# Attention and a state-space layer on one core: fifteen late rotations off TensorE, their first half on ScalarE or GpSimd, the sum on GpSimd

## The chip, the cores and the metric

The kernel runs on one core of one Trainium2 chip. The metric is the time of one execution in device microseconds (us), as the median of several runs; a profile of one execution is taken beside it. TensorE (PE) multiplies matrices into PSUM, VectorE (DVE), ScalarE (ACT) and GpSimd (POOL) work on elements, SyncE (SP) issues transfers. Each engine works off its own queue in order, and semaphores order the engines among themselves.

## The reference

Two layers run on inputs of 2048 tokens by 448 features, and their outputs are put side by side. The first is attention with 16 heads of 28 features, in which a token sees itself and seven tokens at steps of two behind it. The second is a linear recurrence with 448 complex states (S5).

```python
def _A_ref(x, wqkv, wo):
    ...
    logits = jnp.einsum("bhsd,bhswd->bhsw", q, kg) * scale
    attn = _softmax(logits, axis=-1)
    o = jnp.einsum("bhsw,bhswd->bhsd", attn, vg)
    return (o, transposed and flattened) @ wo

def _B_ref(x, Lambda_re, Lambda_im, B_re, B_im, C_re, C_im, log_dt, Dskip):
    Lam_bar = jnp.exp(dt * Lam)
    Bu = jnp.einsum("bld,pd->blp", x + 0j, B_bar)
    for t in range(L):
        h = Lam_bar[None, :] * h + Bu[:, t, :]
        hs.append(h)
    y = 2.0 * jnp.einsum("blp,dp->bld", hseq, Cmat).real + x * Dskip
```

## The kernel before

The order of all work is written out by hand in the string ORDER (from L32): 559 steps such as `W_30@0` or `z52.`. A loop at the end of the kernel calls a function for each. The digits are its arguments, the digit behind @ is the PSUM bank (one of eight), and a last `.` or `=` says whether ScalarE or VectorE copies a result out of PSUM (all these copies go through the helper at L114). A step stands in the queue of the engine that runs it at its place in ORDER, so ORDER sets the queues of all engines.

Attention comes first: projections (QK, QS, V_), products of queries and shifted keys on VectorE (P, L372: two tensors in SBUF), their sums by head on TensorE (E_), softmax (sma, smb, smc). The weights are laid out as bands: AL shifts them on TensorE, `al` copies them into Ak0 or another buffer, `ad` writes them to DRAM and `sp` reads them back skewed into PT. AV multiplies PT with the values (L505), `av` copies the result, W_ multiplies with wo (L518), `w` copies and `ow` stores.

The recurrence treats its 448 complex states as seven groups g of 64, real parts in 64 partitions and imaginary parts in the other 64. Time is cut in blocks of four tokens (j = 0 to 3). BU multiplies inputs with B, BR and UP carry the state inside a block (z and y copy out of PSUM; z takes j, and j = 3 goes to the tile Z3, the others to Z). A scan over blocks follows on VectorE, two groups at a time: `sa` turns the phase (products of tensors in SBUF), `sb` scans, `sd` turns back. DN and `dn` (L754) then finish the even blocks of the group. From these block states the states at j = 0, 1, 2 are made by a rotation: the state before the block, times a complex number that differs by state, is added to Z[g, j]. It is done in one of two ways:

- on TensorE: H_(j, g), a matmul with a rotation matrix (L761), and `h` (L766), by which VectorE adds the result in PSUM to Z[g, j];
- off TensorE, for the nine rotations of groups 4, 5 and 6: `sw(g)`, two transfers (L784, L785), puts a copy of the states with real and imaginary halves exchanged into what is left of BT. Then VectorE makes `ha` or `ka` (L790), t = state x cosine part + Z, into one of five F32 buffers that lie in Ak0, and `hb` or `kb` (L794), Z = exchanged state x sine part + t. The two names of each half are the same code. Both halves read two tensors in SBUF.

C(j, ct) (L825) multiplies Z or Z3 for a quarter ct of the blocks with Cw, over all seven groups, so a C with j below 3 needs all seven rotations of its j. `c` (L831) adds x times Dskip (made by `xd`, L815, in xnB) and empties the bank; `oc` stores. CH is the half of one C, and comes with ch and oh. Cw is scaled on the way by `ca` (ScalarE, L657) and `cs` (VectorE, L661).

On ScalarE the steps `ts` make sine tables, `tx` and `smb` use the exponential. PT is cleared by GpSimd (L895), whose last work are four small copies (L773, step pk).

Of the kernel before, what the change touches and what calls it, by code (L numbers as in the profile page):

```python
# [10 lines left out]
F32 = mybir.dt.float32  # L11
ALU = mybir.AluOpType
ACTF = mybir.ActivationFunctionType
# [16 lines left out]


ORDER = """  # L32
WU@0 XI0@12 xi30. xi20. PP@3 pcopy xi00= pa pb XI1@45 xi31. pd_ xi01. tf3 xi21. pc QS10@6 ts03 pe XH1@7 xh1. qk010.
XA11@3 xa11. tf0 ts13 XA10@2 xt1 ts23 pf xa10= QS00@1 qk000= P000 QK050@04 QK031@57 ts00 QK021@26 QK051 qk050. qk051.
QK061@13 QK060 qh011. pg ts10 qh001. QK030 tf1 ts01 QK020 qk020. QS01@0 qk030= ts20 QK041@45 qh000= V_011@12 P001
QK040 ts11 qk031. qk021. ts21 qk040. tf5 ts05 V_010 V_100@76 qh010. QS11@4 tf4 ts15 P040 P021 v010. P041 v011. xt2
qk041. P020 ts25 tz ts04 V_101 qk001. V_111@31 v101. rb0 V_001@25 V_000 P030 v001. V_110 v110. rb3 QK110@06 v000.
qk011. E_00@5 P050 E_02 E_04 P031 v111. QK161@32 v100. ts14 QK111 qk111. P010 QK121@41 hc0 QK160 qk110. tf6 qh111.
QK120 QK130@76 qh110. QK100@02 ts06 QK101 QK131 ts16 qk121. qk120. qh101. qk101. P011 E_01@1 E_03 P060 P051 E_05
V_401@42 qk130= P061 ts24 qh100. qk100. QK141@73 E_06 QK140 lt01 tf2 qk131. P100 V_400 lt00 ts26 xt3 P130 qk140. ts02  # L40
BD v400. P111 TR0@0 P131 P110 v401. tr0. V_410@16 qk141. V_500@57 xt0 ts12 V_511@42 V_501 V_411 QK151@03 v410. P101
v500. QK150 V_510 P120 v411. hc1 OZ v501. ts22 qk150. E_10@1 E_11@5 sma0 E_13 qk151. BU301@67 v510. v511. BU401@03
BU201@42 BU300 BU200 P121 P151 smb0 LC z30. P140 BR31 XR ci3. z20. P141 ci0. BU400 ci1. CD1 BR21 BU000@64 z21. E_12
z40. E_14 z31. ci2. P150 E_15 BU311@20 P160 P161 BU001 smc0 E_16 lt10 lt11 BU310 BR32 TR1@7 CD2 z00. BR01 z32. tr1.
BU210@15 BR41 xd1 CD3 BR33 BU101@62 sma1 z41. CD0 OP pm0 BU211 AL0@7 al0. BU100 pm3 smb1 ad0 xd3 pm1 z33= BR22 z10.
z22. BU500@37 z01. BR11 z11. BU010@61 smc1 UP3 BU011 wo ca6 tx rb1 BU501 BU111@42 y3= z50. BR02 z02= ca3 BU110 sp0 cs3
xd2 BR12 z12. BR23 AL1@3 z23. al1. BR03 z03. BR13 z13. ad1 pm4 AL2@0 al2. cs6 UP2 y2. BR51 z51. AL3@6 UP1 xd0 y1= al3.
UP0 y0. ca1 BU410@43 BU611@05 BU601@76 BU411 ad2 BU511@21 sa0 BR42 BU600 ca4 BU510 z60. BR52 pm2 cs1 sb0 z42. BR43
BR61 sd0 BU610 DN0@7 sp1 z43. UP4 z52. BR53 z61. ca0 sa2 BR62 z62. AV010@4 y4. z53. av010. AV031@2 AV020@6 rb2 cs4
av031. AV000@0 av020. av000. ad3 AV021@3 AV001@4 av021. sp2 AV011@2 AV030@6 dn0 av030. H_00@7 av001. W_30@0 av011.  # L50
BR63 UP5 sb2 H_20@3 pk H_10@6 W_31@4 y5. W_01@2 sd2 cs0 h20 w31. DN2@1 sp3 w30. W_21@3 h10 z63. w01. w21. ca2 ca5
W_10@4 DN3@6 W_20@0 ow30 UP6 ow01 w10. sa4 y6. dn3 AV131@2 sb4 AV101@3 av101. AV120@6 dn2 AV100@1 ow21 AV130@4 AV110@5
w20. AV111@3 ow31 sd4 h00 ow10 sa6 AV121@0 av120. sb6 sd6 av110. DN5@7 ow20 av111. W_11@6 av121. av131. DN1@5 dn1
H_13@3 W_61@0 av100. dn5 H_12@2 w61. W_51@1 cs2 cs5 sw5 ow61 H_22@5 h13 w11. ha25 DN6@7 W_00@0 ow11 av130. DN4@6 h22
W_70@4 H_11@3 dn4 sw4 ha15 w51. H_03@1 w00. dn6 C32@0 c32 ow00 ha26 W_50@5 hb25 w50. W_40@6 W_71@7 H_21@0 ha16 w70.
W_41@5 ow51 w40. ow70 h11 ha14 W_60@4 h12 ow40 sw6 w41. ow41 h03 hb15 w71. hb14 h21 C30@6 hb16 H_02@3 H_23@5 ow71 h23
ka04 hb26 C33@7 ha24 hb24 C13@2 H_01@1 h01 w60. c33 oc32 C31@4 kb04 oc33 c31 C10@0 C11@5 c11 ka05 oc31 C22@1 c22 h02
c30 ka06 C20@7 ow50 oc11 kb05 ow60 C21@4 kb06 C12@5 c20 oc30 oc20 oc22 c12 C03@1 c21 c10 oc21 oc12 C02@3 oc10 c13 oc13
C01@6 c03 oc03 c01 c02 C00@7 c00 CH1@5 oc01 oc02 CH0@4 oc00 ch1 oh1 ch0 oh0
"""  # L60

@with_exitstack
def kernel(
# [17 lines left out]
    V = nc.vector  # L81
    ACT = nc.scalar
    PE = nc.tensor
    POOL = nc.gpsimd
# [5 lines left out]
    def pool(name, side="left", bufs=1, c=ctx):  # L90
        return c.enter_context(tc.tile_pool(name=name, bufs=bufs, side=side, reuse_waits="tile"))
# [129 lines left out]
    Ak0 = smp.tile([128, 2, 2560], BF16, tag="Ak0")  # L221
# [7 lines left out]
    pp = {}  # L229
# [301 lines left out]
    def small(name, *shape):  # L531
        return const.tile([128, *shape], F32, tag=name, name=name)
# [72 lines left out]
    BT = keep.tile([128, G, 4, 128], BF16, tag="BT")  # L605
# [162 lines left out]
    co2 = small("co2", 2, T - 1, G)  # L768
# [9 lines left out]
    def prev(g, a=0, b=128):  # L778
        s = late["Z3"][a:b, g, OD - 1:OD - 1 + N2]
        return bass.AP(s.tensor, s.offset, [list(s.ap[0]), [EV - OD + 1, 2], [1, N2]])  # L780
# [3 lines left out]
        SP.dma_start(swp(g)[0:64], prev(g, 64, 128))  # L784
        SP.dma_start(swp(g)[64:128], prev(g, 0, 64))  # L785

    def rot_a(e, j, g):
        t = pp["ht", j, g] = Ak0.rearrange("p k n -> p (k n)").bitcast(F32)[:, 512 * (late["k"] % 5):512 * (late["k"] % 5) + 512]
        late["k"] += 1
        e.scalar_tensor_tensor(t.rearrange("p (a n) -> p a n", a=2), prev(g), co2[:, 0, j, g:g + 1],  # L790
                               late["Z"][:, g, j, :].rearrange("p (a n) -> p a n", a=2), ALU.mult, ALU.add)

    def rot_b(e, j, g):
        e.scalar_tensor_tensor(late["Z"][:, g, j, :], BT[:, g].rearrange("p b n -> p (b n)"), co2[:, 1, j, g:g + 1],  # L794
                               pp.pop(("ht", j, g)), ALU.mult, ALU.add)

    @op
    def ha(j, g):
        rot_a(V, j, g)

    @op
    def hb(j, g):
        rot_b(V, j, g)

    @op
    def ka(j, g):
        rot_a(V, j, g)

    @op
    def kb(j, g):  # L810
        rot_b(V, j, g)

    @op
    def xd(cb):
# [47 lines left out]
    late = {}  # L862
# [12 lines left out]
    @op  # L875
    def OP():
        cl.close()
        s6 = pool("a_pt")
        for n, shape in (("PT", (NS, H // HS, PW)), ("oT", (2, 4, 2, 512)), ("wo", (4, D)), ("ya", (6, D))):
            late[n] = s6.tile([128, *shape], BF16, tag=n, name=n)  # L880

        late["Ak"] = [Ak0[:, 0], Ak0[:, 1], late["oT"][:, 1].rearrange("p a b n -> p (a b n)")[:, 0:2560],
                      late["ya"].rearrange("p k n -> p (k n)")[:, 0:2560]]
        late["n"] = 0
        late["k"] = 0

    @op
    def pm(i):
# [14 lines left out]
    for step in ORDER.split():  # L903
        name, args, bank, e = re.fullmatch(r"([A-Za-z]+_?)(\d*)@?(\d*)([.=]?)", step).groups()
# [33 lines left out]
```

## Time and profile before

| | |
|---|---|
| median of 3 runs | 130.98 us (130.95 to 131.43) |
| the profiled execution | 131.52 us, of which the span from first to last instruction is 129.8 us |
| granted clock of TensorE | 1.000 |
| rotations as matmuls, L761 | 12 of 128x512, 4.1 us busy, 0.215 us apart |
| their sums, L766 | 12, 8.1 us busy, 686 ns each |
| first halves, L790 | 9, 6.7 us busy, 746 ns each |
| second halves, L794 | 9, 6.6 us busy, 749 ns each |
| GpSimd | 23.0 us busy, nothing after 73.6 us until the end |
| swap to landing (L784, L785) | 2.1 us |

Busy times are of one profiled execution; an instruction's duration overlaps the next one's by some 0.09 us on VectorE and by more on TensorE, so busy times are above what a queue takes at full speed. A chain of waits is the work that ended last, followed back from the end.

### The profile page before, as it was taken

To read this page: it belongs to the slowest core of one execution; us is meant where nothing else is said; L and a number is where in the kernel's file an instruction comes from. 1 tells how busy PE (TensorE), PEld (TensorE's weight loads), DVE (VectorE), ACT (ScalarE), POOL (GpSimd) and SP (SyncE) were. 2 spreads that over 40 slices of the span, in tenths; PEclk is the share of its full clock that TensorE was granted. 3 is DMA by queue.
4 is the path that set the end of the run, shared out by engine and by line. 5 is a ranking of instruction groups with operands and counts; after the bars stand their busy time and mean duration, and the time that the engine had idled before them with its cause. 6 is when DMAs were issued, how large, how long until landed. Compare 5 with 4: busy or idle time off the path is not lost.

```text
span 129.8 us, 2885 instructions
## 1 busy us (share of the span) xinstructions
PE 122.5 (94%) x1067; PEld 63.4 (49%) x1078; DVE 119.5 (92%) x213; ACT 89.3 (69%) x183; POOL 23.0 (18%) x45
## 2 busy tenths in 40 slices
PE   6889999999999999999999996999999999999990
PEld 6742434434335434434536342955965554555560
DVE  5797999999999999999999999978999999999981
ACT  3589889888879899987899989859997250000000
POOL 6808000000000000037899600000000000000000
PEclk9999999999999999999999999999999999999999
DMA  3899998999999999566458989958211354015272
GB/s 111 201 314 280 310 191 168 224 225 241 159 230 210 216 171 345 205 123 128 165 168 144 326 232 261 219 106 186 99 56 36 110 170 123 7 41 172 83 235 71
DMA packets 44981, 22.91 MB, mean 177 GB/s; under 512 B 31335, under 2 KB 43943, under 8 KB 44967
## 3 DMA queue, kind: packets, MB, share of 16 engines
q1 hardware_dynamic: 44904, 22.72, 74.1%
q8 instruction: 8, 0.13, 0.5%
q14 instruction: 6, 0.05, 0.1%
q10 hardware_dynamic: 63, 0.01, 0.0%
HBM read 11.56 MB, written 6.29 MB: 138 GB/s over the span
## 4 chain that ended last, share of the span: by engine, by line
PE 79%; DMA 7%; ACT 6%; DVE 2%; issue 2%; SPq 1%; ACTq 0%; DVEq 0%
PE ps L238 32%; PE ps L825 15%; PE ps L518 9%; PE ps L505 6%; PE ps L384 4%; DMA pd<-Ak 3%; DMA PT<-pd 3%; PE ps L256 2%; PE ps L761 2%; ACT ctmp L657 2%; PE ps L695 1%; ACT Z L114 1%; PE ps L845 1%; SPq L474 1%; PE ps L341 1%
## 5 line engine op out<-in xcount | busy, mean ns | idle before, releaser
L372 DVE TENSOR_TENSOR pr<-qf,kf 128x2048 bf16<-128x2048 bf16 x24 | 28.0, 1219 | 0.3
L238 PE MATMUL ps<-xbuf,BT 128*128 128x512 bf16 (+1 forms) x108 | 23.4, 380 | 0.4 <-issue 0.3
L238 PE MATMUL ps<-xT,wq 128*128 128x512 bf16 (+1 forms) x92 | 20.5, 380 | 0.5 <-issue 0.2
L825 PE MATMUL ps<-Cw,Z 128*128 128x448 bf16 x105 | 20.6, 353 | 0.0
L114 ACT CAST Z<-ps 128x512 bf16<-128x512 f32 (+1 forms) x31 | 14.8, 525 | 1.3 <-PE ps L695 1.1
L825 PEld LDWEIGHTS <-Z 128*128 128x128 bf16 x105 | 10.3, 98 | 10.0 <-DVE Z L794 0.4
L238 PEld LDWEIGHTS <-BT 128*128 128x128 bf16 (+1 forms) x112 | 8.9, 97 | 12.0 <-issue 2.9
L518 PE MATMUL ps<-wo,oT 128*128 128x448 bf16 x64 | 13.7, 353 | 0.0
L238 PEld LDWEIGHTS <-wq 128*128 128x128 bf16 (+1 forms) x96 | 7.6, 97 | 11.6 <-issue 3.6
L895 POOL MEMSET PT<- 128x4320 f32 x3 | 11.1, 3702 | 10.2 <-PE ps L388 10.2
L238 PE MATMUL ps<-wq,xT 128*128 128x448 bf16 (+1 forms) x64 | 12.4, 353 | 0.0
L114 ACT CAST ya<-ps 128x448 bf16<-128x448 f32 (+1 forms) x17 | 8.7, 551 | 5.2 <-PE ps L518 3.6
L114 ACT CAST oT<-ps 128x512 bf16<-128x512 f32 x17 | 9.1, 621 | 1.1 <-PE ps L505 1.1
L505 PE MATMUL ps<-PT,v_s 128*32 128x135 bf16 (+1 forms) x256 | 8.7, 299 | 1.2 <-DMA PT<-pd 1.2
L657 ACT ACTIVATE ctmp<-Cw,c2t 64x448 f32<-64x448 bf16 x14 | 9.3, 666 | 0.2
L831 DVE TENSOR_TENSOR xbuf<-ps,xnB 128x448 bf16<-128x448 f32 x15 | 8.7, 618 | 0.4 <-PE ps L825 0.4
L518 PEld LDWEIGHTS <-oT 128*128 128x128 bf16 x64 | 6.3, 98 | 5.5 <-ACT oT L114 0.2
L766 DVE TENSOR_TENSOR Z<-ps,Z 128x512 bf16<-128x512 f32 x12 | 8.1, 686 | 0.9 <-PE ps L761 0.9
L114 ACT CAST v_s<-ps 128x448 bf16<-128x448 f32 x16 | 7.9, 547 | 1.0 <-PE ps L238 0.9
L238 PEld LDWEIGHTS <-xT 128*128 128x128 bf16 (+1 forms) x64 | 5.4, 97 | 5.8 <-issue 1.2
L505 PEld LDWEIGHTS <-v_s 128*32 128x32 bf16 x256 | 7.0, 111 | 1.9 <-issue 1.5
L114 ACT CAST qf<-ps 128x512 bf16<-128x512 f32 x11 | 6.4, 592 | 0.8 <-PE ps L238 0.7
(159 smaller groups left out, 199.6 us busy)
## 6 DMA issues: line engine op xcount, KB each, us to landing
PT<-pd SPq DMA_DIRECT2D x16, 156.0 KB, 3.9
xnB<-in_B_x_dram SPq DMA_DIRECT2D x2, 896.0 KB
out_dram<-ya SPq DMA_DIRECT2D x16, 112.0 KB, 1.8
out_dram<-xbuf SPq DMA_DIRECT2D x15, 112.0 KB, 1.7
pd<-Ak SPq DMA_DIRECT2D x2, 640.0 KB, 5.3
xbuf<-in_A_x_dram SPq DMA_DIRECT2D x2, 448.0 KB
xnB<-in_B_x_dram SPq DMA_DIRECT2D x4, 224.0 KB, 5.8
xnB<-in_B_x_dram SPq DMA_DIRECT2D x4, 192.0 KB, 4.5
```

The costliest lines, as they stand in the source:

```text
L114: (ACT.copy if e == "A" else V.tensor_copy)(o, i)
L238: PE.matmul(o, l, r, start=(first and i == 0), stop=(not first and i == len(pairs) - 1 and not more[s]))
L256: PE.matmul(p[:, 0:128], wz[:], wz[:], start=True, stop=True)
L372: V.tensor_tensor(t[:], q.unsqueeze(1).to_broadcast((128, 4, 512)), k4, ALU.mult)
L384: PE.matmul(acc[s][32 * i:32 * i + 32], E[:, f, ws, :], t[:, i, :], start=(f == 0 and ws == 0), stop=False)
L505: PE.matmul(p[32 * hh:32 * hh + 32, 128 * bl:128 * bl + n], v_s[:, t, 4 * hg + hh, :], PT[:, t % NS, (4 * hg + hh) // HS, (4 * hg + hh) % ...
L518: PE.matmul(p[:, 0:D], late["oT"][:, b // 4, hg, par, 128 * (b % 4):128 * (b % 4) + 128], late["wo"][:, hg, :], start=(hg == 0), stop=(hg ...
L657: ACT.activation(t[a:a + 64, 0:D], Cw[b:b + 64, g, :], ACTF.Copy, scale=c2t[a:a + 64, g:g + 1])
L766: V.tensor_tensor(zz, pp.pop(("h", j, g))[:], zz, ALU.add)
L825: PE.matmul(p[:, 0:D], z, Cw[:, g, :], start=(g == 0), stop=(g == G - 1))
L831: V.tensor_tensor(yo, pp.pop(("c", j, ct))[:, 0:D], xnB[:, ct, j, :], ALU.add)
L895: POOL.memset(late["PT"][:, 4 * i:4 * i + 4].rearrange("p t g n -> p (t g n)").bitcast(F32), 0.0)
```

## The change

Fifteen rotations instead of nine are made off TensorE: those of groups 2 to 6. Groups 0 and 1 stay on TensorE. A rotation off TensorE is now three steps: its first half is a product alone, by ScalarE (`ga`, groups 4 to 6) or by GpSimd (`gp`, groups 2 and 3); GpSimd adds Z to it in place (`gb`); VectorE makes the second half (`hb`) as before. Two more pairs of `sw` transfers are issued. A buffer now belongs to its rotation by the order in which first halves stand in ORDER, still five in turn.

```diff
-    def rot_a(e, j, g):
-        t = pp["ht", j, g] = Ak0.rearrange("p k n -> p (k n)").bitcast(F32)[:, 512 * (late["k"] % 5):512 * (late["k"] % 5) + 512]
-        late["k"] += 1
-        e.scalar_tensor_tensor(t.rearrange("p (a n) -> p a n", a=2), prev(g), co2[:, 0, j, g:g + 1],
+    def ht(j, g):
+        if (j, g) not in hts:
+            hts[j, g] = Ak0.rearrange("p k n -> p (k n)").bitcast(F32)[:, 512 * (len(hts) % 5):512 * (len(hts) % 5) + 512]
+        return hts[j, g]
+
+    @op
+    def ha(j, g):
+        V.scalar_tensor_tensor(ht(j, g).rearrange("p (a n) -> p a n", a=2), prev(g), co2[:, 0, j, g:g + 1],
                                late["Z"][:, g, j, :].rearrange("p (a n) -> p a n", a=2), ALU.mult, ALU.add)
...
     @op
     def hb(j, g):
-        rot_b(V, j, g)
...
+        V.scalar_tensor_tensor(late["Z"][:, g, j, :], BT[:, g].rearrange("p b n -> p (b n)"), co2[:, 1, j, g:g + 1],
+                               ht(j, g), ALU.mult, ALU.add)
+
+    @op
+    def ga(j, g):
+        ACT.activation(ht(j, g).rearrange("p (a n) -> p a n", a=2), prev(g), ACTF.Copy, scale=co2[:, 0, j, g:g + 1])
+
+    @op
+    def gp(j, g):
+        POOL.tensor_scalar(ht(j, g).rearrange("p (a n) -> p a n", a=2), prev(g), co2[:, 0, j, g:g + 1], 1.0, ALU.mult, ALU.mult)
+
+    @op
+    def gb(j, g):
+        POOL.tensor_tensor(ht(j, g), ht(j, g), late["Z"][:, g, j, :], ALU.add)
```

`ha` stays defined and is not called. ORDER is replaced as a whole. By count of its steps: H_ and h 12 to 6; ha and ka 9 to 0; hb and kb 9 to 15; gp 6, ga 9 and gb 15 are new; sw 3 to 5. Copies that change their engine: al0, al1, al3, av030, av130, v000, w31, w40, w70, xa11, xi21, y5, z01, z03 and z50 go from ScalarE to VectorE; qh000, qk030, qk130, xa10, y1, y3 and z33 go the other way. The steps ts05, ts15 and ts25, which make the last sine table, now stand late, ts15 and ts25 behind tx. The late part of the new order, from the first AV (every rotation of groups 2 to 6 lies in it):

```
AV000@7 AV030@0 av030= AV020@4 av000. z62. cs1 y4. AV010@7 av010. AV001@6 AV011@2 AV021@3 z53. AV031@7 UP5 av001.
av020. y5= av011. DN3@6 dn3 BR63 W_00@4 sp2 W_10@2 av031. av021. W_11@0 z63. gp23 gb23 DN2@7 sa4 dn2 sb4 W_31@3 w31=
w00. gp13 w10. W_30@5 UP6 ca4 cs4 W_01@6 w11. ca0 gp12 w30. W_21@4 sp3 AV111@2 gp22 gb12 cs0 AV110@7 AV100@0 AV101@3
av111. sd4 y6. sw3 ca2 gp03 gb03 AV121@5 sa6 av121. ow10 AV130@2 av130= av101. ow00 ow11 sb6 AV131@1 av110. AV120@5
DN4@3 ow30 gb22 gb13 av131. DN5@2 W_51@7 hb23 ca5 W_61@1 av120. ow31 dn4 cs2 W_20@3 av100. sw2 dn5 hb12 W_71@2 w20.
hb13 hb03 w51. cs5 w71. H_11@5 ow51 h11 W_70@0 H_21@3 ow20 w70= sw5 W_40@7 sd6 ga15 gb15 ow71 ow70 W_41@2 ga05 C32@5
w01. h21 w61. sw4 H_01@6 hb22 gb05 H_10@0 C33@1 w40= w41. ow41 DN6@2 ga14 h10 dn6 ga16 h01 hb15 H_00@3 ga24 C31@7
W_60@0 gb14 hb14 h00 W_50@2 ow01 sw6 hb05 c32 ga26 w60. gb16 oc32 ga04 gb24 H_20@6 ow60 hb16 gb26 ga25 C30@0 ow40
C10@3 w21. gb25 xd1 w50. ow50 hb24 C11@5 C12@4 c31 hb26 c10 C13@2 oc31 hb25 ga06 gb06 oc10 h20 CH1@7 c12 C21@3 oc12
gb04 ow61 xd3 c30 hb04 gp02 oc30 C22@6 gb02 C20@4 c21 c11 oc21 oc11 hb02 c33 ch1 oh1 hb06 C00@0 c00 oc33 c20 oc20 c22
c13 C03@3 C02@5 oc00 c03 oc13 oc03 C01@1 ow21 c02 oc02 c01 oc22 oc01 CH0@7 ch0 oh0
```

In the order before, the first AV was AV010, and ha25, the first half rotation off TensorE, stood behind h13 near the middle of the same part; H_13, H_12, H_22, H_03, H_02 and H_23 stood between DN1 and C33.

More of the change, by code (lines that the diff above doesn't have):

```diff
@@ L32 @@
 ORDER = """
[L33 to L57, printed above, removed]
@@ L58 @@
-c30 ka06 C20@7 ow50 oc11 kb05 ow60 C21@4 kb06 C12@5 c20 oc30 oc20 oc22 c12 C03@1 c21 c10 oc21 oc12 C02@3 oc10 c13 oc13
-C01@6 c03 oc03 c01 c02 C00@7 c00 CH1@5 oc01 oc02 CH0@4 oc00 ch1 oh1 ch0 oh0
+WU@0 XI0@12 xi00= xi20. xi30. PP@3 pcopy pa pb XI1@45 xi01. xi21= xi31. QS10@6 qk010. XA11@7 pc pd_ tf3 pe xa11=
+XA10@1 XH1@3 QS00@2 qk000= xa10. xh1. P000 QS01@0 P001 pf QK050@45 pg rb1 qk001. QK051 tf6 QK031@67 qk050. ts03
+QK021@13 ts13 ts23 QK041@20 BD QK040 qk040. P040 tf0 qk041. QK030 qk030. qk051. QK020 qk020. QS11@4 QK061@20 V_111@65
@@ new lines @@
+ts06 ts16 ts26 ts00 qk011. P041 QK060 qh010. P020 ts10 V_110 P021 qk021. v110. v111. P011 V_100@14 tz tf1 E_00@3
+qk031. E_02 E_04 qh011. V_011@65 ts20 rb3 qh001. V_101 v101. V_001@70 V_000 v001. V_010 v100. ts01 QK110@40 v010.
+QK111 qh000. QK161@16 P010 v011. qk111. v000= P050 ts11 ts21 qk110. QK121@72 QK160 tf2 xt3 qh110. qh111. QK120
+QK100@50 hc0 QK130@46 qh101. QK101 qk121. qh100. P031 hc1 QK131 tf4 ts04 xt0 qk100. E_01@2 qk130. xt2 P030 qk120.
+qk101. ts02 E_03 P051 E_05 V_410@15 V_411 P061 rb0 qk131. QK141@47 QK151@06 P060 E_06 lt00 P101 ts12 lt01 QK150 P110
@@ new lines @@
+ts22 v411. qk151. QK140 TR0@3 qk140. V_500@25 tr0. V_501 v410. P131 tf5 xt1 P100 ts14 ts24 v501. qk150. V_401@64 v500.
+V_511@31 V_510 v511. v510. pk P130 V_400 LC P111 E_11@5 E_10@0 E_13 sma0 BU301@21 qk141. v400. P120 P150 BU401@37
+v401. BU201@64 BU300 ts05 smb0 XR OZ z30. BU200 z20. BU400 ci0. P151 BR31 P141 ci1. z31. P140 z40. P121 BU000@26 BR21
+E_12 E_14 z21. E_15 BU311@13 ci3. BU001 P160 P161 E_16 BU310 smc0 CD3 BR32 ci2. lt10 lt11 TR1@4 CD0 z00. tr1. BR01
+z01= sma1 BU210@05 BU211 BU101@24 AL0@6 BU100 al0= CD2 rb2 z32. BR33 smb1 BR41 z10. BR22 CD1 OP pm0 z22. smc1 BU010@16
@@ new lines @@
+ad0 BR11 ca6 z41. pm3 wo BU500@20 BU501 pm1 cs6 BU011 z50= z11. BU111@74 BU110 BR12 ca3 xd0 BR02 sp0 z33. z12. BR51
+z02= AL1@2 BR23 BR13 UP3 z23. BR03 z13. y3. pm4 tx al1= AL2@7 UP1 y1. z03= AL3@1 ad1 UP0 UP2 al2. y0. xd2 ts15 al3=
+BU410@23 BU601@47 BU411 sa0 z51. cs3 y2. BU611@61 ad2 BU511@05 sb0 sd0 ca1 BU600 z60. BR42 z42. BU510 BR61 BR43 sa2
+BR52 BU610 DN0@4 ts25 z43. sp1 DN1@2 dn0 UP4 z61. ad3 BR62 sb2 dn1 sd2 z52. pm2 BR53 AV000@7 AV030@0 av030= AV020@4
+av000. z62. cs1 y4. AV010@7 av010. AV001@6 AV011@2 AV021@3 z53. AV031@7 UP5 av001. av020. y5= av011. DN3@6 dn3 BR63
@@ new lines @@
+W_00@4 sp2 W_10@2 av031. av021. W_11@0 z63. gp23 gb23 DN2@7 sa4 dn2 sb4 W_31@3 w31= w00. gp13 w10. W_30@5 UP6 ca4 cs4
+W_01@6 w11. ca0 gp12 w30. W_21@4 sp3 AV111@2 gp22 gb12 cs0 AV110@7 AV100@0 AV101@3 av111. sd4 y6. sw3 ca2 gp03 gb03
+AV121@5 sa6 av121. ow10 AV130@2 av130= av101. ow00 ow11 sb6 AV131@1 av110. AV120@5 DN4@3 ow30 gb22 gb13 av131. DN5@2
+W_51@7 hb23 ca5 W_61@1 av120. ow31 dn4 cs2 W_20@3 av100. sw2 dn5 hb12 W_71@2 w20. hb13 hb03 w51. cs5 w71. H_11@5 ow51
+h11 W_70@0 H_21@3 ow20 w70= sw5 W_40@7 sd6 ga15 gb15 ow71 ow70 W_41@2 ga05 C32@5 w01. h21 w61. sw4 H_01@6 hb22 gb05
@@ new lines @@
+H_10@0 C33@1 w40= w41. ow41 DN6@2 ga14 h10 dn6 ga16 h01 hb15 H_00@3 ga24 C31@7 W_60@0 gb14 hb14 h00 W_50@2 ow01 sw6
+hb05 c32 ga26 w60. gb16 oc32 ga04 gb24 H_20@6 ow60 hb16 gb26 ga25 C30@0 ow40 C10@3 w21. gb25 xd1 w50. ow50 hb24 C11@5
+C12@4 c31 hb26 c10 C13@2 oc31 hb25 ga06 gb06 oc10 h20 CH1@7 c12 C21@3 oc12 gb04 ow61 xd3 c30 hb04 gp02 oc30 C22@6 gb02
+C20@4 c21 c11 oc21 oc11 hb02 c33 ch1 oh1 hb06 C00@0 c00 oc33 c20 oc20 c22 c13 C03@3 C02@5 oc00 c03 oc13 oc03 C01@1
+ow21 c02 oc02 c01 oc22 oc01 CH0@7 ch0 oh0
@@ L785, in sw @@
         SP.dma_start(swp(g)[64:128], prev(g, 0, 64))
-    def rot_a(e, j, g):
-        t = pp["ht", j, g] = Ak0.rearrange("p k n -> p (k n)").bitcast(F32)[:, 512 * (late["k"] % 5):512 * (late["k"] % 5) + 512]
-        late["k"] += 1
[L790 to L795, printed above, removed]
+    def ht(j, g):
+        if (j, g) not in hts:
+            hts[j, g] = Ak0.rearrange("p k n -> p (k n)").bitcast(F32)[:, 512 * (len(hts) % 5):512 * (len(hts) % 5) + 512]
+        return hts[j, g]
+    hts = {}
     @op
     def ha(j, g):
-        rot_a(V, j, g)
+        V.scalar_tensor_tensor(ht(j, g).rearrange("p (a n) -> p a n", a=2), prev(g), co2[:, 0, j, g:g + 1],
+                               late["Z"][:, g, j, :].rearrange("p (a n) -> p a n", a=2), ALU.mult, ALU.add)
     @op
     def hb(j, g):
-        rot_b(V, j, g)
-    @op
-    def ka(j, g):
-        rot_a(V, j, g)
-    @op
-    def kb(j, g):
-        rot_b(V, j, g)
+        V.scalar_tensor_tensor(late["Z"][:, g, j, :], BT[:, g].rearrange("p b n -> p (b n)"), co2[:, 1, j, g:g + 1],
+                               ht(j, g), ALU.mult, ALU.add)
+    @op
+    def ga(j, g):
+        ACT.activation(ht(j, g).rearrange("p (a n) -> p a n", a=2), prev(g), ACTF.Copy, scale=co2[:, 0, j, g:g + 1])
+    @op
+    def gp(j, g):
[3 more added lines that the diff above has]
+        POOL.tensor_tensor(ht(j, g), ht(j, g), late["Z"][:, g, j, :], ALU.add)
     @op
@@ L884, in OP @@
         late["n"] = 0
-        late["k"] = 0
     @op
```

## The prediction

> **What bounds the kernel now.** I read the page's shares first, then busy time by stretches of 10 us, the chain of waits, and last the single instructions of VectorE and GpSimd where the two overlap.
>
> ```profile
> PE 122.5 (94%) x1067; PEld 63.4 (49%) x1078; DVE 119.5 (92%) x213; ACT 89.3 (69%) x183; POOL 23.0 (18%) x45
> ```
>
> Two engines are nearly full. The stretches (columns: length; PE, PEld, DVE, ACT, POOL busy; clock; DMA) show where:
>
> ```profile
> 90.00:100.00 10.00, 9.99 (x193) 6.90 (x191) 9.63 (x24) 9.46 (x19) 0.00 (x0) 1.00 0.22 68
> 100.00:110.00 10.00, 10.00 (x54) 5.03 (x52) 10.00 (x18) 2.86 (x7) 0.00 (x0) 1.00 0.42 126
> 110.00:120.00 10.00, 10.00 (x54) 5.08 (x53) 9.96 (x18) 0.00 (x0) 0.00 (x0) 1.00 0.25 80
> ```
>
> From 90 us TensorE and VectorE are both full at clock 1.00, ScalarE empties at 106.8 and GpSimd does nothing. The chain says which ends last:
>
> ```profile
> 81.07 3.86 PE ps L505 x108
> ...
> 100.31 0.43 PE ps L761 x2
> ...
> 110.81 14.57 PE ps L825 x77
> 125.38 1.36 PE ps L845 x14
> 126.76 0.39 DVE xbuf L854
> ```
>
> From the first AV at 81.07 it runs on TensorE nearly throughout. So TensorE sets the end, but VectorE, which makes what the C products read and empties their banks, has next to no slack.
>
> **Part 1, six rotations leave TensorE.** Six of the twelve H_ matmuls (L761) go; in the chain two of them take 0.43 us, so 6 x 0.215 = 1.3 us. From the first AV to the end TensorE's steps, by their spacing, sum to 44.6 us instead of 46.0.
>
> **Part 2, VectorE.** Neighbours overlap by some 0.09 us, so I count spacing, not duration: 0.66 us for a half rotation, 0.60 for h, 0.53 for c or w.
>
> ```profile
> 110.69 0.75 DVE L790 SCALAR_TENSOR_TENSOR Ak<-Z,co,Z 128x512 f32<-128x512 bf16 x1
> 111.34 0.75 DVE L794 SCALAR_TENSOR_TENSOR Z<-BT,co,Ak 128x512 bf16<-128x512 bf16 x1
> 112.01 0.76 DVE L790 SCALAR_TENSOR_TENSOR Ak<-Z,co,Z 128x512 f32<-128x512 bf16 x1
> ```
>
> In the late queue six h go (-3.6), nine first halves go (-5.9), six second halves come (+4.0); the new order adds three w copies (+1.6) and two av copies (+1.2) from ScalarE and moves xd1 and xd3 from about 70 us to the end (+2.0). Net -0.7 us: VectorE stays as full as it was.
>
> **Part 3, GpSimd.** Six gp and fifteen gb, in the order gp23 gb23 gp13 gp12 gp22 gb12 and so on to gb02. No row shows either operation. GpSimd copies are nearest:
>
> ```profile
> 6.42 0.39 POOL L214 COPY wq<-wq 64x256 bf16<-64x256 bf16 x1
> 9.96 0.61 POOL L215 COPY wq<-wq 64x512 bf16<-64x512 bf16 x1 [3.15 <-DMA wq<-in_A_wqkv_dram]
> ```
>
> 256 more elements cost 0.22 us: 0.85 ns each after 0.17 us of start. A gp reads 512: 0.61 us. A gb reads 1024: at least 0.61 (if its two reads go side by side), 1.04 if one after the other, and 1.6 at the costliest slope on GpSimd's rows (affine selects, 0.239 us for 48 elements and 0.532 for 256: 1.41 ns). I take 1.04: two tensors are read. All 21 then need 6 x 0.61 + 15 x 1.04 = 19.3 us. The first can start after dn3, near 85.5 us (DN3 stands 4.1 us of TensorE's work behind the first AV, which I put at 81.0); without waits GpSimd would be through at 105. Needed: hb14 to hb16 at C10 (28.7 us of TensorE's work behind the first AV: 109.7), the g of j=2 at 115.0, of j=0 at 119.7. Alone the queue is early enough. The question is whether it runs beside VectorE for nothing.
>
> **Part 4, the two together.** The trace shows that it doesn't:
>
> ```profile
> 10.99 1.23 DVE L372 TENSOR_TENSOR pr<-qf,kf 128x2048 bf16<-128x2048 bf16 x1
> ```
>
> ```profile
> L218 POOL COPY wq<-wq x2: 288/785/1282, 11.1 to 12.4; 64x128 bf16<-64x128 bf16 x2
> ```
>
> ```profile
> 5.89 0.16 DVE L556 SCALAR_TENSOR_TENSOR f<-dt,P 128x7 f32<-128x7 f32 x1
> ...
> 6.48 0.35 DVE L567 SCALAR_TENSOR_TENSOR fT<-km,fT 128x7 f32<-128x7 f32 x1
> ```
>
> ```profile
> 72.48 0.42 DVE L114 CAST Z<-ps 128x256 bf16<-128x256 f32 x1
> 73.13 0.42 DVE L721 TENSOR_TENSOR p<-Z,tab 64x512 bf16<-64x512 bf16 x1 [0.22 <-ACT Z L114]
> ```
>
> ```profile
> L773 POOL COPY co<-co x4: 198/200/379, 72.5 to 73.2; 64x21 f32<-64x21 f32 x4
> ```
>
> Of two equal GpSimd copies (L218) the one beside VectorE's product of two SBUF tensors took 1.28 us, not 0.29. The other way round, a scalar_tensor_tensor of 7 columns (L567), 0.16 us elsewhere, took 0.35 while the GpSimd copy from 6.42 ran, and ended 0.02 us behind it. Of the four copies L773, those beside a VectorE copy out of PSUM took 0.20, the one beside L721 (two SBUF inputs) 0.38. So a GpSimd operation that reads SBUF and a VectorE operation with two SBUF inputs exclude each other; PSUM-fed ones run on.
>
> By the kind of operands hb, cs, xd, the scans, sa and sd are of the excluded kind: 22.1 us of VectorE's queue between dn3 and hb06. PSUM-fed (dn, w, av, h, c) are 11.9 us. Of GpSimd's time I count only the reading, since the long L218 copy ended 0.15 us after the product, less than its own 0.29: 6 x 0.435 + 15 x 0.87 = 15.7 us. PSUM-fed stretches after the last addition (c30 to ch1, 2.4 us) can't serve; of the other 9.5 I let three quarters, 7.1 us, hide GpSimd, since it will at times stand still for a buffer. The rest, 15.7 - 7.1 = 8.6 us, VectorE waits. With 0.61 us for a gb it is 21 x 0.435 - 7.1 = 2.0; with 1.6 us, and all 9.5 used, 6 x 0.435 + 15 x 1.44 - 9.5 = 14.7.
>
> [...]
>
> What queues behind the new waits: hb23, hb12, hb13 and hb03 (each waits for GpSimd) stand ahead of sd6 on VectorE, and C32, at 102 us, needs sd6. hb14 to hb16 stand ahead of the c that empty TensorE's banks. Scratch is five buffers, so ga15 waits for hb23, ga05 for hb13, and so on: behind the ga on ScalarE stand copies of W products (w60, w50, w21) whose banks TensorE wants. The round trip hb, ga or gp, gb, hb then stalls all engines in step, so I let none of the 8.6 us vanish in slack.
>
> **Part 5, what I cost at nothing.** Nine ga on ScalarE: the nearest row is ctmp, 0.67 us for 448 columns, so some 0.72 each, 6.5 us; they hide in the 7 us idle of 100 to 110 and in what follows; uncovered, they would delay the w copies by as much. Two more sw pairs: four issues of 0.6 us on SP ahead of the output stores, landing 2.1 us after; SP has room, hb23 stands several us behind sw3; exposed, 2.4 us. The new order before 81 us: adding rows in queue order up to the copy al1, with which the way to the first AV begins, VectorE has 63.4 us of work instead of 63.6; I keep 81.0, give or take 0.5. ScalarE gets a fourth table load (1.28 us in the rows there are), as ts25 now follows tx, near 78 us; al0, al1 and al3 leave it (1.8 us) and cover that.
>
> **Sum.** VectorE paces the end then, so its saving of 0.7 counts and the 1.3 of TensorE does not: -0.7 + 8.6 = +7.9 us. The profiled execution took 131.5 us (span 129.8 and 1.7 around it), 0.5 above the median of 130.98: 131.5 + 7.9 - 0.5 = 138.9 us.
>
> **Rivals.**
> *Faster: no exclusion that costs.* If the read phases interleave, or gaps within VectorE's operations suffice, hb is never late, since the queue alone ends at 105 against 109.7. TensorE's 1.3 us then counts: 129.7. For it: single, short collisions are all that the trace shows, and GpSimd's memsets (3.70 us each, all three) are never stretched, but they read nothing. Against it: both directions are there.
> *Weak exclusion*: gb at 0.61 us, 2.0 us of waiting, 132.3. For it: no row of a GpSimd addition. Against: a gb reads two tensors, one of them F32.
> *Heavier*: h and c, with one SBUF input beside PSUM, exclude too, or gb takes 1.6 us: 14.7 - 0.7, 145. No row bears on h and c.
> *No change*: nothing excluded, but the table load delays sa4 and dn4 by its 1.28 us and takes the gain back: 131.0. Against it: ScalarE gives up 1.8 us just before.
> That the change does not do what it says is not open: L761 halves, L790 is gone and GpSimd has 21 new instructions.
>
> **How the numbers follow.** Forecast (133 to 143) 0.64, weak 0.07, heavier 0.06, faster rival 0.18, no change 0.05. About 0.5% is what can be told from no change here: 130.3 to 131.6. Faster 0.18, same 0.05, slower 0.64 + 0.07 + 0.06 = 0.77. The likeliest case's own range is 133 to 143; for all, 129.5 reaches the faster rival and 145 the upper bound.
>
> **What would show it.** Right: hb, cs, sd or xd with durations well over their 0.75, 0.68, 0.42 and 1.09 us, or gaps before them ended by POOL; gp and gb stretched over their shortest; PE below 9.5 in 10 between 95 and 125; C32, C10 and CH1 late. Wrong: hb at 0.75 throughout and PE at 10.0 to the end (faster rival); a gb's shortest near 0.6 (weak); h or c stretched (heavier); TensorE's first AV later than 81.5 (the order, not the halves).

## The result and the profile after

The changed kernel takes 141.63 us (median of 4 runs, 141.21 to 142.31) against 131.09 us for the kernel before on the same chip: 1.0805 times, 95% interval 1.0749 to 1.0861. That is 10.5 us more; 138.9 us was predicted. The profile below is of the longest of the four (142.31 us).

The page of the profiled execution, with the slices of three engines and of TensorE's clock:

```profile
span 140.6 us, 2908 instructions
...
PE 125.8 (89%) x1072; PEld 62.8 (45%) x1072; DVE 130.4 (93%) x212; ACT 93.4 (66%) x185; POOL 50.6 (36%) x66
...
PE   6999999999999999999999799992599598949891
...
DVE  5789999999999999999999998999998999999882
...
POOL 6819200000000000839970004997005448991000
PEclk9999999999999999999999999998569999999999
```

VectorE is as full as before, now over a longer span. TensorE has holes from the 28th slice (95 us) on, in or shortly behind the stretches in which GpSimd is busy; from 84 to 95 us, where GpSimd is busy too, it is still full. The columns of the next rows are those of the prediction (length; PE, PEld, DVE, ACT, POOL busy; clock; DMA), and the stretches are the same, with one more behind them:

```profile
90.00:100.00 10.00, 5.73 (x165) 4.11 (x164) 9.74 (x14) 7.58 (x14) 7.32 (x7) 0.88 0.24 71
100.00:110.00 10.00, 9.26 (x37) 4.10 (x36) 9.20 (x16) 4.64 (x9) 2.76 (x3) 0.78 0.18 54
110.00:120.00 10.00, 8.36 (x44) 4.15 (x45) 10.00 (x14) 4.32 (x8) 5.78 (x5) 1.00 0.25 72
120.00:130.00 10.00, 8.05 (x47) 4.32 (x46) 10.00 (x13) 0.88 (x2) 6.94 (x5) 1.00 0.27 89
```

From 90 to 100 us TensorE works 5.7 us where it worked 9.99, while VectorE is busy for 9.74 us with 14 instructions instead of 24. What they are, from VectorE's timeline and then GpSimd's:

```profile
93.81 1.27 DVE L722 TENSOR_TENSOR p<-hs,tab 64x512 bf16<-64x512 bf16 x1
95.10 1.28 DVE L723 TENSOR_TENSOR p<-hs,tab 64x512 bf16<-64x512 bf16 x1
96.40 1.28 DVE L743 TENSOR_TENSOR vv<-hs,tab 128x512 bf16<-128x512 bf16 x1
97.72 0.42 DVE L744 TENSOR_TENSOR Z<-vv,p 128x512 bf16<-128x512 bf16 x1
```

```profile
93.39 4.01 POOL L815 TENSOR_TENSOR Ak<-Ak,Z 128x512 f32<-128x512 f32 x3
```

These are the four instructions of sd4. Beside three gb the first three take 1.27 to 1.28 us each, and the fourth takes 0.42 us as GpSimd is done at 97.4. One of them gets through for each gb, three of each between 93.4 and 97.7 us: the two engines take turns here. If they shared the reading at half speed each, 0.42 us would become 0.84, not 1.27. The groups of VectorE after 85 us show which operations suffer (busy us, mean ns of one):

```profile
L802 DVE SCALAR_TENSOR_TENSOR Z<-BT,co,Ak 128x512 bf16<-128x512 bf16 x15 | 14.0, 953 | 0.0
L835 DVE TENSOR_TENSOR xbuf<-ps,xnB 128x448 bf16<-128x448 f32 x15 | 8.7, 614 | 1.1 <-PE ps L829 1.1
L767 DVE TENSOR_TENSOR Z<-ps,Z 128x512 bf16<-128x512 f32 x6 | 4.1, 681 | 0.6 <-PE ps L762 0.6
L662 DVE SCALAR_TENSOR_TENSOR Cw<-Cw,c1t,ctmp 128x448 bf16<-128x448 bf16 x4 | 4.1, 1040 | 0.0
```

In the kernel before, the groups of cs and c were these (hb and h are in the table above):

```profile
L661 DVE SCALAR_TENSOR_TENSOR Cw<-Cw,c1t,ctmp 128x448 bf16<-128x448 bf16 x7 | 4.7, 678 | 0.0
L831 DVE TENSOR_TENSOR xbuf<-ps,xnB 128x448 bf16<-128x448 f32 x15 | 8.7, 618 | 0.4 <-PE ps L825 0.4
```

hb (L802) and cs (L662), with two inputs in SBUF, rose from 749 and 678 ns to 953 and 1040. c (L835) and h (L767), with one input in PSUM, took 614 and 681 ns, against 618 and 686 before.

GpSimd's own instructions (shortest, median and longest in ns):

```profile
L815 POOL TENSOR_TENSOR Ak<-Ak,Z x15: 1150/1336/2072, 87.0 to 125.9; 128x512 f32<-128x512 f32 x15
```

```profile
L811 POOL TENSOR_SCALAR Ak<-Z,co x6: 852/1053/1125, 86.1 to 124.7; 128x512 f32<-128x512 bf16 x6
```

And the chain that ended last, on TensorE nearly throughout before, runs mostly on VectorE behind 84.7 us (TensorE still has 100.1 to 106.5 us of it and the last C products from 132.4 us):

```profile
90.62 0.52 DVE ya L115
91.14 2.65 DVE Cw L662 x2
93.81 1.27 DVE p L722
...
114.20 2.22 DVE Z L802 x2
...
126.36 1.61 DVE xnB L819
```

### The profile page after: what moved, and what is told of

Read it like the earlier page. It is cut to its first block, busy times and chain, and to the rows that moved or that the text cites. A ratio compares the mean times of both kernels' runs of the same rounds, so it can differ in the third digit from the quotient of the medians.

```text
span 140.6 us, 2908 instructions
## 1 busy us (share of the span) xinstructions
PE 125.8 (89%) x1072; PEld 62.8 (45%) x1072; DVE 130.4 (93%) x212; ACT 93.4 (66%) x185; POOL 50.6 (36%) x66
## 4 chain that ended last, share of the span: by engine, by line
PE 55%; DVE 27%; DMA 9%; issue 4%; SPq 3%; DVEq 0%
PE ps L239 33%; DVE Z L802 6%; PE ps L519 4%; PE ps L385 4%; PE ps L829 3%; DMA pd<-Ak 3%; DMA xbuf<-in_A_x_dram 3%; DVE xbuf L835 3%; DMA PT<-pd 3%; PE ps L506 3%; DVE p L723 2%; DVE p L722 2%; PE ps L696 2%; DVE Cw L662 2%; DVE xnB L819 2%
## 5 line engine op out<-in xcount | busy, mean ns | idle before, releaser
L815 POOL TENSOR_TENSOR Ak<-Ak,Z 128x512 f32<-128x512 f32 x15 | 20.8, 1401 | 14.3 <-ACT Ak L807 14.1
L829 PE MATMUL ps<-Cw,Z 128*128 128x448 bf16 x105 | 21.2, 353 | 2.8 <-DVE Z L744 1.5
L239 PE MATMUL ps<-xT,wq 128*128 128x512 bf16 (+1 forms) x96 | 20.0, 380 | 0.0
L519 PE MATMUL ps<-wo,oT 128*128 128x448 bf16 x64 | 15.3, 392 | 0.0
L115 ACT CAST Z<-ps 128x512 bf16<-128x512 f32 (+1 forms) x30 | 13.8, 508 | 1.1 <-PE ps L239 0.5
L802 DVE SCALAR_TENSOR_TENSOR Z<-BT,co,Ak 128x512 bf16<-128x512 bf16 x15 | 14.0, 953 | 0.0
L239 PEld LDWEIGHTS <-wq 128*128 128x128 bf16 (+1 forms) x96 | 7.6, 97 | 10.9 <-issue 3.2
L115 ACT CAST ya<-ps 128x448 bf16<-128x448 f32 x13 | 6.6, 541 | 6.2 <-PE ps L519 6.1
L811 POOL TENSOR_SCALAR Ak<-Z,co 128x512 f32<-128x512 bf16 x6 | 6.0, 1002 | 13.0 <-ACT oT L115 13.0
L807 ACT ACTIVATE Ak<-Z,co 128x512 f32<-128x512 bf16 x9 | 6.1, 723 | 6.2 <-DVE Z L755 4.2
L115 ACT CAST oT<-ps 128x512 bf16<-128x512 f32 x15 | 8.0, 606 | 2.6 <-PE ps L506 2.5
L835 DVE TENSOR_TENSOR xbuf<-ps,xnB 128x448 bf16<-128x448 f32 x15 | 8.7, 614 | 1.1 <-PE ps L829 1.1
```

The lines of the kernel that those rows point to most:

```text
L115: (ACT.copy if e == "A" else V.tensor_copy)(o, i)
L239: PE.matmul(o, l, r, start=(first and i == 0), stop=(not first and i == len(pairs) - 1 and not more[s]))
L519: PE.matmul(p[:, 0:D], late["oT"][:, b // 4, hg, par, 128 * (b % 4):128 * (b % 4) + 128], late["wo"][:, hg, :], start=(hg == 0), stop=(hg ...
L802: V.scalar_tensor_tensor(late["Z"][:, g, j, :], BT[:, g].rearrange("p b n -> p (b n)"), co2[:, 1, j, g:g + 1], ht(j, g), ALU.mult, ALU.add)
L807: ACT.activation(ht(j, g).rearrange("p (a n) -> p a n", a=2), prev(g), ACTF.Copy, scale=co2[:, 0, j, g:g + 1])
L815: POOL.tensor_tensor(ht(j, g), ht(j, g), late["Z"][:, g, j, :], ALU.add)
```

## The experiments

Three series, each on one chip; a ratio is to the kernel before, timed on that chip (131.9, 132.2 and 131.5 us). "On the first chip's scale" is a ratio times 131.09 us.

### GpSimd writes, but doesn't read

```diff
-        POOL.tensor_scalar(ht(j, g)..., prev(g), co2[:, 0, j, g:g + 1], 1.0, ALU.mult, ALU.mult)
+        POOL.memset(ht(j, g), 0.0)
...
-        POOL.tensor_tensor(ht(j, g), ht(j, g), late["Z"][:, g, j, :], ALU.add)
+        POOL.memset(ht(j, g), 0.0)
+        POOL.memset(ht(j, g), 0.0)
```

> Left out: GpSimd's products (gp) and its additions of Z (gb). In their place GpSimd writes the same buffers with memsets, one for a gp and two for a gb, so that its queue, its waits and about its time stay, but it reads nothing. Theory (a GpSimd operation that reads SBUF and a VectorE operation with two SBUF inputs exclude each other): hb falls from 953 ns back to 0.75 us on the mean, no VectorE operation is stretched, TensorE's gap at 95 to 100 us closes, and the time is 129.5 to 130.5 us. Rival (the new order, its buffer ring and the longer chain of steps are slow by themselves): hb at 0.75 us too, but the time stays above 136 us.

Measured: 0.9959 times the kernel before (0.9922 to 0.9996), 130.6 us on the first chip's scale. VectorE's busy time is below that of the kernel before, and hb is back:

```profile
PE 122.3 (95%) x1063; PEld 63.1 (49%) x1072; DVE 118.3 (92%) x212; ACT 93.5 (73%) x185; POOL 42.1 (33%) x81
...
L802 DVE SCALAR_TENSOR_TENSOR Z<-BT,co,Ak 128x512 bf16<-128x512 bf16 x15 | 10.8, 739 | 0.0
```

Two memsets take 1.05 us, nearly a gb's shortest 1.15, in the same queue and with the same waits on the buffers. The whole loss is gone, and VectorE's busy time falls from 130.4 to 118.3 us. The 12.1 us between the two busy times are the stretch.

One thing changes besides the reading: memsets don't wait for Z. Those of the first five rotations ran from 73.3 to 81.1 us, whereas the first gp of the changed kernel started at 86.1. The memsets of the ten later rotations (100.3 to 115.4 us) stand ahead of their hb as the additions do, nine of them behind ScalarE's products, and all fifteen hb took 739 ns on the mean (the row above). So the order and the ring cost nothing to speak of, nor does the longer chain for these ten; for the first five this run leaves it open, and the run with unused additions, below, has no chain.

### VectorE makes the first halves itself

`gb` becomes the former `ha` on VectorE; `ga` and `gp` issue nothing.

> The whole computation, in the changed order: VectorE makes the first half with Z added, as before, at the place of each gb; ga and gp are gone and GpSimd is idle. VectorE has 15 x 0.66 = 9.9 us more work of its own and no exclusion. Theory (a gb costs VectorE about 1 us of waiting): 134 to 138 us, faster than the changed kernel although VectorE does all the work itself. Rival (VectorE's own load is the bound and GpSimd does relieve it): 142 us or more.

Measured: 1.0587 times (1.0515 to 1.0660), 138.8 us on the first chip's scale: above the expected 134 to 138 us, but below the changed kernel's 1.0805, and the intervals don't meet. hb took 740 ns on the mean. (ScalarE is relieved too, of its nine products.) GpSimd's help costs VectorE more than the 9.9 us of work that it takes over.

### The order of before, with nine additions on GpSimd

```diff
     def rot_a(e, j, g):
...
-        e.scalar_tensor_tensor(t..., prev(g), co2[:, 0, j, g:g + 1], late["Z"][:, g, j, :]..., ALU.mult, ALU.add)
+        ACT.activation(t..., prev(g), ACTF.Copy, scale=co2[:, 0, j, g:g + 1])
+        POOL.tensor_tensor(t, t, late["Z"][:, g, j, :], ALU.add)
```

> The kernel before with its order, nine rotations off TensorE and twelve on it; only the nine first halves are made by ScalarE (the product) and GpSimd (the addition of Z). VectorE gets 9 x 0.66 = 5.9 us less work of its own. Theory: hb well above 0.75 us, GpSimd's additions above 1.15 us, and 131 to 134 us, that is no gain in spite of the 5.9 us. Rival (the new order is what costs): hb at 0.75 us and 130.5 to 131.1 us.

Measured: 1.0108 times (1.0031 to 1.0185), 132.5 us on the first chip's scale. The time is as expected, the reason isn't:

```profile
L794 DVE SCALAR_TENSOR_TENSOR Z<-BT,co,Ak 128x512 bf16<-128x512 bf16 x9 | 6.7, 762 | 3.0 <-DMA BT<-Z 2.0 <-POOL Ak L791 1.1
```

hb is hardly stretched. It stands idle for 3.0 us instead, for the swapped copy and for GpSimd: what is left for the additions to fall on is time in which VectorE stood idle (3.15 us from 100 to 110 us, 2.12 from 110 to 120), and h, dn and c, which they didn't hinder (681, 413 and 618 ns on the mean, 686, 415 and 618 before). And the chain got longer. This run shows that a longer chain can cost by itself in an order made for a shorter one; it says nothing for exclusion.

### TensorE kept busy

```diff
     def DN(g):
         p = pp["dn", g] = ps()
+        if g == 4:
+            for _ in range(18):
+                PE.matmul(p[:], wz[:], late["Z"][:, 0, 0, :], start=True, stop=True)
```

> The changed kernel and 18 matmuls of no use ahead of DN4, where TensorE stands idle from 95.5 us; their result is overwritten. If the clock that the profile shows at 0.5 from 97.6 to 104.5 us comes of that idle time, it stays at 1.00 and the W matmuls behind it are 0.19 us apart instead of 0.37. VectorE is busy for most of those 5 us, so the theory gives 140.3 to 141.3 us: the slow clock is a consequence that costs below 1.3 us. Rival (the slow clock is a main part of the loss): below 139.5 us.

Measured: 1.0753 times (1.0677 to 1.0830), 141.0 us on the first chip's scale, as expected. The clock stayed at 1.00 where it had fallen to half, but it fell later (0.83 on the mean from 120 to 130 us). Against the changed kernel's 1.0805 on one chip and 1.0790 on another the difference isn't resolved. A main part of the loss it isn't; a small cost of the slow clock stays open, the more so as this run has a slow stretch too.

### The changed kernel again, and its products on ScalarE

> The changed kernel once more, unchanged, so that the others of this series can be set against it on one chip. Expected: 1.07 to 1.09 times the kernel before, TensorE's clock at 0.5 for 3.4 or 6.8 us somewhere after 95 us.

Measured: 1.0790 times (1.0737 to 1.0844). The repetition agrees.

In the other run, `gp` uses the line of `ga`, so that only the fifteen additions stay on GpSimd.

> The whole computation, in the changed order; the six products that GpSimd made (gp) are made by ScalarE, the fifteen additions stay on GpSimd. Theory: each gp no longer excludes VectorE, some 0.7 us of its 0.85 each, so 4 us of the 12 us by which VectorE's operations are stretched go, and the time falls to 137 to 139 us, or 1.045 to 1.06 times the kernel before; hb stays near 0.95 us. Rival (the additions and the waits for them are all that counts): within 1 us of the changed kernel.

Measured: 1.0532 times (1.0481 to 1.0583), 138.1 us on the first chip's scale, as expected. VectorE's busy time is 127.0 us: 3.4 of the 12.1 us of stretch are gone, 0.6 us for each product taken off GpSimd, and the time falls by as much (1.0790 to 1.0532 is 3.4 us). hb stood at 1008 ns. So gp, with one tensor input, cost VectorE time too.

### ScalarE's products and VectorE's additions, in both orders

GpSimd does nothing; ScalarE makes both products of a rotation in BF16, and VectorE adds both to Z. First in the new order with fifteen rotations, then in the order of before with nine.

```diff
...
     def gb(j, g):
-        POOL.tensor_tensor(ht(j, g), ht(j, g), late["Z"][:, g, j, :], ALU.add)
+        V.tensor_tensor(late["Z"][:, g, j, :], late["Z"][:, g, j, :], ht(j, g), ALU.add)
...
     def hb(j, g):
...
+        ACT.activation(t, BT[:, g].rearrange("p b n -> p (b n)"), ACTF.Copy, scale=co2[:, 1, j, g:g + 1])
+        V.tensor_tensor(late["Z"][:, g, j, :], late["Z"][:, g, j, :], t, ALU.add)
```

> The whole computation, in the changed order, without GpSimd: ScalarE makes both products of each of the fifteen rotations in BF16, and VectorE adds them to Z one after the other, as additions of BF16 tensors in SBUF (0.42 us each in the rows of sa and sd, 0.34 apart, so 0.68 for a rotation instead of 0.66 for hb alone). VectorE's own work is then that of the run with memsets plus 0.3 us, nothing is excluded, and the theory gives 129.5 to 131.5 us on the first chip, 0.99 to 1.005 times the kernel before. Rival (ScalarE's 30 products of 0.72 us, 21.6 us in place of 6.5, now come late, the copies of W behind them): 134 us or more.

> The kernel before with its order, nine rotations off TensorE; both products of each by ScalarE in BF16 and two additions of BF16 tensors by VectorE. VectorE has 9 x (1.32 - 0.68) = 5.8 us less work of its own, TensorE as much as before. Since TensorE ends last there, the theory gives no gain above 0.5 us: 0.995 to 1.005 times the kernel before. Rival (VectorE is what ends last in the kernel before): 2 us or more faster.

Measured: 1.0378 times (1.0326 to 1.0430) and 1.0106 times (1.0066 to 1.0145); both expectations missed. In the first the rival named there came true: ScalarE was full where its copies were needed, and TensorE waited (the row of 90 to 100 us):

```profile
90.00:100.00 10.00, 7.33 (x169) 4.69 (x168) 8.04 (x20) 9.82 (x19) 0.00 (x0) 0.90 0.24 71
```

In the second neither the theory nor its rival came true. TensorE waited 1.10 us for a copy by ScalarE that empties a bank (w60, the row of L114), which stood behind ScalarE's products (L791, L797). The chain, from a product over the swap to the C's that end the kernel:

```profile
105.70 0.63 ACT Ak L791
...
106.85 2.05 DMA BT<-Z
...
111.54 0.61 ACT Ak L797
112.15 0.42 ACT ya L114
112.58 0.04 issue
112.62 14.73 PE ps L828 x77
```

VectorE has room there (7.21 us busy of 10 from 110 to 120), and nothing is gained. Taking work off VectorE was not enough here; whether an order made for the new division of work would gain by it was not tried. No version with the whole computation was found that beats the kernel before.

### Additions that nobody waits for, and their control

Into the kernel before, with its own order, fifteen additions of gb's form are put; their result is not read and no instruction waits for them. The control writes the same tile instead.

```diff
+    @op
+    def gx(j, g):
+        scr = attn.rearrange("p t n -> p (t n)").bitcast(F32)[:, 0:512]
+        a = scr.rearrange("p (a n) -> p a n", a=2)
+        POOL.tensor_tensor(a, prev(g), iot[:].unsqueeze(1).to_broadcast((128, 2, N2)), ALU.add)
```

> The kernel before with its order, and fifteen additions on GpSimd of the form of gb whose result nobody reads and for which no instruction waits, three behind each of dn3, dn2, dn5, dn4 and dn6 (two inputs in SBUF, output into a tile that is dead by then). Theory (exclusion between the reads): VectorE's sa, sd, scans, cs, ha and hb are stretched, its PSUM-fed copies and sums are not; each addition of 1.15 us excludes VectorE for about 1 us unless it falls on PSUM-fed work, so 15 x 1.0 less a third to a half hidden: 7 to 10 us of stretch, and 5 to 10 us more time, 1.04 to 1.08 times the kernel before. Rival (the loss comes of waits on a longer chain, not of GpSimd's reading beside VectorE): 0.995 to 1.005 times, nothing stretched.

> The control to the run with idle additions: at the same places GpSimd writes the same dead tile with two memsets of 512 F32 in a row (1.05 us together), after a one-element operation that makes it wait for dn as the additions do. Theory: no VectorE operation is stretched by more than 0.2 us in all but a few places, and the time is 0.995 to 1.005 times the kernel before. Rival (any work of GpSimd slows VectorE, whether it reads or not): the stretch and the time of the run with additions.

Measured: 1.0644 times (1.0566 to 1.0721), 8.4 us on the first chip's scale, for the additions; 0.9995 times (0.9963 to 1.0028) for the writes. Groups of VectorE behind 88 us with additions:

```profile
L794 DVE SCALAR_TENSOR_TENSOR Z<-BT,co,Ak 128x512 bf16<-128x512 bf16 x9 | 8.3, 935 | 0.0
L790 DVE SCALAR_TENSOR_TENSOR Ak<-Z,co,Z 128x512 f32<-128x512 bf16 x9 | 8.1, 894 | 0.0
L766 DVE TENSOR_TENSOR Z<-ps,Z 128x512 bf16<-128x512 f32 x10 | 6.7, 677 | 0.0
L736 DVE TENSOR_TENSOR_SCAN hs<-rk,vv 128x256 bf16<-128x256 f32 x3 | 2.8, 973 | 0.0
```

The same groups with writes:

```profile
L766 DVE TENSOR_TENSOR Z<-ps,Z 128x512 bf16<-128x512 f32 x10 | 6.7, 681 | 0.0
L790 DVE SCALAR_TENSOR_TENSOR Ak<-Z,co,Z 128x512 f32<-128x512 bf16 x9 | 6.7, 742 | 0.0
L794 DVE SCALAR_TENSOR_TENSOR Z<-BT,co,Ak 128x512 bf16<-128x512 bf16 x9 | 6.5, 742 | 0.0
L736 DVE TENSOR_TENSOR_SCAN hs<-rk,vv 128x256 bf16<-128x256 f32 x3 | 2.0, 678 | 0.0
```

VectorE's busy time rose from 119.5 to 127.9 us with the additions, by the 8.4 us that the kernel got longer. (The profiled execution, with a mean granted clock of 0.975, has a span 9.5 us longer.) Exclusion is shown here without any wait on GpSimd's result: no chain, no ring, no new order.

The writes are a weaker control than was meant. GpSimd's first and last start (shortest, median and longest in ns before them), additions and then writes:

```profile
L801 POOL TENSOR_TENSOR attn<-Z,iot x15: 1121/1400/1494, 90.4 to 114.4; 128x512 f32<-128x512 bf16 x15
```

```profile
L802 POOL MEMSET attn<- x15: 524/525/527, 74.2 to 95.8; 128x512 f32 x15
```

The one element that the control reads ahead of its writes lies in the part of Z3 that dn doesn't write, so the control didn't wait for dn and was through by 96.4 us, ahead of the first ha and hb. What ran beside its writes are the scans, sa, sd and cs, and none of them is stretched: behind 88 us three scans took 678 ns on the mean, two cs 676, and the four instructions of the sd of groups 4 and 5 420 to 427. For hb beside writes the run with memsets stands (739 ns on the mean).

## Why the prediction was right, and where it was off

**What bounds, and part 1.** Right: TensorE's 1.3 us counted for nothing, since VectorE paced the late part. Where GpSimd doesn't read, the change is worth 0.4% (0.9959).

**Part 2, VectorE's own work.** Net -0.7 us predicted. Without stretch VectorE's busy time is 118.3 us against 119.5: -1.2.

**Part 4, exclusion.** Right in kind, by three runs: it goes when GpSimd stops reading, falls by 3.4 of 12.1 us when six products leave GpSimd, and appears in the kernel before when unused additions are put in. Right on which operations too: h and c are not touched (681 and 614 ns), which ends the heavier rival's first form; gb's 1.15 us ends the second, a gb of 1.6.

**The size.** The forecast was +7.9 us, the measurement +10.5. The term that was mis-sized is VectorE's waiting, 8.6 us predicted and 12.1 measured; with -1.2 of own work that makes 10.9, close to the 10.5 of the median. Most of it is part 3's price of GpSimd's operations: a gb took 1.15 us at its shortest, not 1.04, and a gp 0.85, not 0.61. In the prediction's own formula, with its 0.17 us of start taken off each, 15 x 0.98 + 6 x 0.68 = 18.8 us of reading stand in place of 15.7. What is hidden then is 18.8 - 12.1 = 6.7 us, where 7.1 were allowed. That these agree is in part luck: the trace has only about 5.0 us of GpSimd's gp and gb beside PSUM-fed work of VectorE (c 2.4, h 1.3, copies 0.9, dn 0.4), so the rest was hidden in another way. A gp has one tensor input, as a copy has, and cost 0.24 us more than the copy of its size: the nearest row was too kind.

**The whole duration or the read phase.** If a gb and VectorE's operation kept each other out for their whole durations, a gb (1.15 us alone) and an operation of 0.42 us would take 1.57 us together. In the alternation from 93.8 us the three start 1.29 and 1.30 us apart. So some 0.3 us of each pair overlap, as the prediction assumed from the L218 copies. With whole durations at the measured lengths its formula would give 6 x 0.85 + 15 x 1.15 - 7.1 = 15.3 us, and 12.1 were measured.

**Part 5.** The costs set at nothing were hidden: the first AV ran at 80.60 us (81.0 predicted), and the run with memsets, which has the table load, the extra swaps and ScalarE's nine products (0.72 us each, as estimated), lost nothing by them in sum.

**The rivals.** The faster one fell with the stretched hb, the weak one with gb's 1.15 us, no change with both. The prediction's sign that TensorE would stand below 9.5 in 10 from 95 us came true. What it left out is the clock, below, whose part in the 10.5 us stays open.

## What to carry to other kernels

An operation moved from VectorE to GpSimd to relieve VectorE must be priced by what VectorE does meanwhile: where that had two inputs in SBUF, a moved addition stretched an operation of 0.42 us to 1.27, by 0.85 us, and VectorE makes such an addition, together with the product, in 0.66. Work beside stretches in which VectorE reads PSUM didn't stretch it (c 614 ns, h 681), though no run here gained time by that; writes cost nothing (0.9995). And look in the profile of before for the few places where the two engines already meet: three short rows foretold this loss.

Two SBUF inputs may not be the only case. In the kernel before, a VectorE instruction with one tensor input met a GpSimd instruction near 6 us:

```profile
6.09 0.29 DVE L565 TENSOR_SCALAR fT<-f 128x7 f32<-128x7 f32 x1
```

```profile
5.95 0.41 POOL L210 TENSOR_SCALAR_AFFINE_SELECT shf<-zt 128x270 bf16<-128x270 bf16 x1
```

L565 ended 0.02 us behind GpSimd's L210; the next of its kind, L566, took 0.16 us. In the changed kernel the instruction that was L565 (L566 there) took 0.21 us and ended 0.03 us behind GpSimd's copy L215. So an operation of VectorE with one tensor input in SBUF isn't safe for that reason alone; which ones are was not tried.

## What was not expected of the hardware

TensorE's granted clock fell in several of these runs. In the changed kernel it was at 0.50 for 6.8 us, from 97.64 to 104.46 us, and twelve W matmuls ran 0.37 us apart instead of 0.19. These are the rows of TensorE before and in that time:

```profile
94.81 0.67 PE L506 MATMUL ps<-PT,v_s 128*32 128x135 bf16 x16
98.20 0.40 PE L749 MATMUL ps<-Z,R 128*128 128x256 bf16 x1 [2.72 <-ACT oT L115]
100.12 0.37 PE L749 MATMUL ps<-Z,R 128*128 128x256 bf16 x1 [1.52 <-DVE oT L115]
100.29 5.06 PE L519 MATMUL ps<-wo,oT 128*128 128x448 bf16 x15
```

The drop came 2.16 us into the gap of 2.72 us that ended at 98.20 us. Gaps of 1.53 and 1.95 us between matmuls, which ended at 110.91 and 125.89 us, had no drop behind them: the clock was 1.00 from 104.5 us to the end of the last C products.

The means of other runs show drops elsewhere. In the repetition the clock was 0.97 from 90 to 100 us and 0.68 from 100 to 110; with ScalarE's products in the new order it was 0.90 and 0.93 there; with VectorE's own first halves, and with TensorE kept busy, it was 0.83 from 120 to 130 us. With all first products on ScalarE it stayed at 1.00 from 80 to 130 us, although TensorE was busy for only 7.03 of the 10 us from 100 to 110. So less work for TensorE in a stretch did not always bring a drop; what brings one, and how long it then lasts, these runs leave open.
